# Parts of the weights' conversion and of k's low half move from VectorE to GpSimd, in short pieces

## The chip, the cores and the metric

The kernel runs on one NeuronCore of a Trainium2 chip. The metric is the device time of one execution in microseconds (us), as the median of several runs. In the profile the engines are PE (TensorE, matmuls), PEld (its weight loads), DVE (VectorE), ACT (ScalarE), POOL (GpSimd) and SP (SyncE, which here only issues DMAs). Each engine works through a queue of its own, strictly in order; semaphores make it wait for the others.

## The reference

Eight batches of attention with 8 heads, 576 positions and 64 columns a head, and behind it a gated MLP. All inputs are float32 in the reference; the two large weights arrive as 64-bit floats, and the kernel reads them as pairs of 32-bit words.

```python
scores = scale * np.matmul(q, k.transpose(0, 1, 3, 2))
cum = np.cumsum(np.maximum(s, 0.0), axis=-1)
bias = -(cum[:, :, :, None] - cum[:, :, None, :])
scores = np.where(causal, -1e9, scores + np.minimum(bias, 0.0))
attn = softmax(scores)                    # max taken off, + 1e-9 under the sum
x = np.matmul(attn, v)                    # heads side by side: 576 x 512
h = np.maximum(x @ w_in, 0.0)             # 512 -> 1024
u, v = h[..., :512], h[..., 512:]
v_n = (v - mean) / sqrt(var + 1e-6)
v_s = einsum('ts,bsd->btd', w_spatial, v_n) + b_spatial
out = (u * v_s) @ w_out                   # 512 -> 512
```

## The kernel before, in words

**Tiling.** Two heads make a pair, four pairs a batch: 32 pairs and 8 MLPs. To keep float32's accuracy with 16-bit matmuls, every operand is split in a high part (the value rounded to float16) and a low part (the value less its high part), and a product is taken as high x high, high x low and low x high.

**A pair.** Its k and q are loaded as `kraw` and `qraw` (`load_raw`, one buffer each, so the next pair's load waits until the last reader of this one's is done). `split_raw` makes the parts: of k, a cast into `KB` (line 251, DVE) and the low part over it (line 255, DVE: 64 partitions x 1152 elements); of q, a cast into `QA` (line 259, ACT) and the low part `QB` (line 264, POOL, by `pieces` at line 239, four instructions of 64 x 288). The first three pairs are native: their scores are taken from `kraw` and `qraw` in float32, without parts. `s_pass` then makes the scores (PE, line 316, seven jobs a pair, into three PSUM banks), adds the mask with the row maximum (DVE, line 320), takes exp (ACT, line 326), and writes the weights' high part (ACT, line 335) and low part (DVE, line 336) into `pb`, which a DMA on SP's queue transposes into `pT` (line 341). `av_pass` multiplies `pT` with v (PE, lines 413 and 423) and splits the result into `xt` (lines 429 and 430).

**The MLP of a batch.** `vps` (PE, line 457, the gate half of w_in), its normalisation (lines 473 to 491: `hv`, BN_STATS on DVE, the inverse root `rs` in two tiny POOL instructions at lines 482 and 483, `vn`), `ups` (line 507), `sps` with w_spatial (lines 520 to 523), the gate `g` (lines 525 to 528) and `ops` with w_out (line 539).

**The weights.** They are converted once, during the first pairs, in 128-row chunks: w_in in 8 (four of the gate half, four of the other), w_out in 4, w_spatial in 4 and a tail. `split_w64` turns 64-bit words into float32 by three DVE instructions (lines 167, 168, 170), squares the upper word on ACT (line 173), sets what is too small to zero on DVE (line 174), and calls `split_w`: the high part on ACT (line 148), and the low part either on DVE (line 150) or, with a scaled copy on ACT (line 152), on POOL (line 153). Which of the two is set by the numbers N_W1 = 2, N_W2 = 1, N_W3 = 5 and N_W4 = 0: DVE makes the low part of three w_in chunks, of all w_spatial chunks and the tail; POOL that of the other five w_in chunks and the four of w_out. w_spatial comes as float32 and goes through `split_w` alone.

**The order.** `plan` gives each step a position; up to position G_END the engines other than PE keep that order among steps marked as first. Beyond that a scheduler sets the order in each queue from its own estimate of when an operand is ready, so a changed engine for one step can move others. "Row" below is a place in an engine's queue, with equal neighbours counted once.

Of the kernel before, what the change touches and what calls it, by code (L numbers as in the profile page):

```python
# [12 lines left out]
ALU = mybir.AluOpType  # L13
# [5 lines left out]
SW = 64.0  # L19
SWSP = 1024.0  # L20
# [10 lines left out]
def attn_gated_mlp(ctx, tc, qT, kT, v, s, w_in, w_spT, b_sp, w_out, outT):  # L31
    nc = tc.nc
    P = 128
# [7 lines left out]
    w_out = w_out.bitcast(U32)  # L41
# [46 lines left out]
    KB = [cp.tile([P, 2, S], F16, name=f"KB{i}") for i in range(3)]  # L88
# [51 lines left out]
    wo1 = cp.tile([P, FC, DM], F16, name="wo1")  # L140
    wo2 = cp.tile([P, FC, DM], F16, name="wo2")
    ws1 = cp.tile([P, NFULL, S], F16, name="ws1")
    ws2 = cp.tile([P, NFULL, S], F16, name="ws2")
    wx1 = cp.tile([P, S], F16, name="wx1")
    wx2 = cp.tile([P, S], F16, name="wx2")

    def split_w(dst1, dst2, raw, sc, dve):
        nc.scalar.activation(dst1, raw, AF.Copy, bias=0.0, scale=sc)
        if dve:
            nc.vector.scalar_tensor_tensor(out=dst2, in0=raw, scalar=sc, in1=dst1, op0=ALU.mult, op1=ALU.subtract)  # L150
            return
        nc.scalar.activation(raw, raw, AF.Copy, bias=0.0, scale=sc)
        nc.gpsimd.tensor_tensor(out=dst2, in0=raw, in1=dst1, op=ALU.subtract)

    def fetch_w64(src, tag_s):
        st = wk.tile([P, 2 * NF], U32, tag=tag_s, bufs=1, name="wst")
        st = st.rearrange("p (f two) -> p f two", two=2)
        nc.sync.dma_start(out=st, in_=src.rearrange("p (f two) -> p f two", two=2))
        return st

    def split_w64(dst1, dst2, st, tag_t, dve):

        n = st.shape[1]
        lo, hi = st[:, 0:n, 0], st[:, 0:n, 1]
        t = wk.tile([P, S], U32, tag=tag_t, bufs=2, name="wt")[:, 0:n] if tag_t != "hv" else \
            wk.tile([P, NF], U32, tag="hv", bufs=2, name="wt")
        nc.vector.tensor_scalar(t, hi, 0x07FFFFFF, 3, op0=ALU.bitwise_and, op1=ALU.logical_shift_left)
        nc.vector.scalar_tensor_tensor(out=t, in0=hi, scalar=0xC0000000, in1=t, op0=ALU.bitwise_and,
                                       op1=ALU.bitwise_or)
        nc.vector.scalar_tensor_tensor(out=t, in0=lo, scalar=29, in1=t, op0=ALU.logical_shift_right,  # L170
                                       op1=ALU.bitwise_or)
        sq, tf = hi.bitcast(F32), t.bitcast(F32)
        nc.scalar.activation(sq, sq, AF.Square, bias=0.0, scale=1.0)
        nc.vector.scalar_tensor_tensor(out=tf, in0=sq, scalar=2.0 ** -30, in1=tf, op0=ALU.is_ge, op1=ALU.mult)
        split_w(dst1, dst2, tf, SW, dve)

    wsts = {}

# [3 lines left out]

    def load_win(hf, c):
        split_w64(win1[:, c, hf * NF:(hf + 1) * NF], win2[:, c, hf * NF:(hf + 1) * NF], wsts.pop((hf, c)),
                  "hv" if hf else "ob", c < (N_W1 if hf else N_W2))

    def load_wout(c):
        split_w64(wo1[:, c], wo2[:, c], fetch_w64(w_out[c * P:c * P + P], "wst"), "ob", c < N_W4)

    def load_wsp(c):  # L190
        st = wk.tile([P, S], F32, tag="ob", bufs=2, name="wsp_st")
        nc.sync.dma_start(out=st, in_=w_spT[c * P:c * P + P])
        split_w(ws1[:, c], ws2[:, c], st, SWSP, c < N_W3)

    def load_wtail():
        s4 = wk.tile([P, S], F32, tag="ob", bufs=2, name="wsx_st")
        nc.sync.dma_start(out=s4[0:TAIL], in_=w_spT[NFULL * P:S])
        nc.sync.dma_start(out=s4[TAIL:2 * TAIL], in_=w_spT[NFULL * P:S])
        split_w(wx1, wx2, s4, SWSP, N_W3 > 4)
        bf = wk.tile([1, S], F32, tag="ob", bufs=2, name="bf")  # L200
        bp = wk.tile([1, 3, S], F16, tag="wst", bufs=1, name="bp")
        nc.sync.dma_start(out=bf, in_=b_sp)
        nc.vector.tensor_scalar(bf, bf, SWSP * SVN / 2048.0, None, op0=ALU.mult)
        for i in range(3):
            nc.vector.tensor_copy(bp[:, i], bf)
            if i < 2:
                nc.vector.tensor_tensor(out=bf, in0=bf, in1=bp[:, i], op=ALU.subtract)
        for i in range(3):
            nc.sync.dma_start(out=wx2[TAIL + i:TAIL + i + 1], in_=bp[:, i])
# [25 lines left out]
    def pieces(eng, out, in0, in1):  # L235
        for j in range(2):
            for hf in range(2):
                c = slice(hf * TH, hf * TH + TH)
                eng.tensor_tensor(out=out[:, j, c], in0=in0[:, j, c], in1=in1[:, j, c], op=ALU.subtract)  # L239

    def split_raw(hb, nm, pr):

        p = 2 * hb + pr
        i = p % 3
        raw = raws[hb, 2 * pr, nm]
        lo, hi = slice(0, 64), slice(64, 128)
        if nm == "k":
            if p < N_CD:
                nc.scalar.copy(KA[i][hi], raw[hi])
            if p < N_KA:  # L250
                nc.vector.tensor_copy(KB[i], raw)
            else:
                nc.scalar.copy(KB[i], raw)
            eng = nc.gpsimd if p < N_KP else nc.vector
            eng.tensor_tensor(out=KB[i][lo], in0=raw[lo], in1=KB[i][lo], op=ALU.subtract)  # L255
            if p >= N_CD:
                nc.sync.dma_start(out=KA[i][hi], in_=KB[i][hi])
        else:
            (nc.scalar.copy if p < N_QA else nc.vector.tensor_copy)(QA[i][hi], raw[hi])  # L259
            if p < N_CD:  # L260
                (nc.scalar.copy if p < N_QA else nc.vector.tensor_copy)(QB[i][lo], raw[lo])
            else:
                nc.sync.dma_start(out=QB[i][lo], in_=QA[i][hi])
            pieces(nc.gpsimd, QB[i][hi], raw[hi], QA[i][hi])
# [311 lines left out]
    for p in range(4):  # L576
        l = (-20, -19, O_R2, O_R3)[p]
        if p < N_NS:
            at(l, True, native_tiles, p)
            at(l, True, native_sel, p)  # L580
            at((-19.9, -18.9, O_S2, O_S3)[p], True, native_cum, p)
        else:
            at(l, True, behind, "c", load_raw, 1, p % 2)
            for nm in "kq":
                at((0, 0, O_S2, O_S3)[p], True, split_raw, 1, nm, p % 2)
# [10 lines left out]
    for hb in range(2, NHB):  # L596
        lag = LAGS if hb < 4 else LAG
        for pr in range(2):
            at(4 * hb + 2 * pr - O_LR + (LAGR if hb < 4 else LAG), False, load_raw, hb, pr)
            at(4 * hb + 2 * pr - O_LD + lag, False, aux_rows, 2 * hb + pr)  # L600
            for n, nm in enumerate("kq"):
                at(4 * hb + 2 * pr - O_LD + lag + D_LD * n, False, split_raw, hb, nm, pr)
        at(4 * hb - O_LV + (LAGV if hb < 4 else LAG), False, fetch_v, hb)
        at(4 * hb - O_LV + (LAGV if hb < 4 else LAG), False, load_v, hb)
    for c in range(KC):
        at(O_WL + D_WL * c, False, fetch_win, 1, c)
        at(O_UL + D_UL * c, False, fetch_win, 0, c)
# [11 lines left out]
    for b in range(B):  # L619
        s0, s1 = 8 * b + O_M + LAG, 8 * b + 8 + O_M + LAG  # L620
        poss = [s0 + (s1 - s0) / NU * k for k in range(NU)]
        if b == 0:
# [5 lines left out]
            n = len(pre)  # L628
# [9 lines left out]
    for pos, _, first, fn, args in plan:  # L638
        n = len(traced)
# [46 lines left out]
```

## Time and profile before

| what | us |
|---|---|
| median of 3 runs | 735.04 (731.93 to 736.01) |
| the profiled execution | 736.15 |
| its span in the trace | 734.4 |
| busy: PE / DVE / ACT / POOL | 633.7 / 606.4 / 525.1 / 186.5 |

The profiled execution is 1.11 us over the median. Its span is the stretch from the first instruction to the last, 1.75 us less than its time. The page gives busy times by engine, the share of the span in 40 slices, and groups of instructions by line; a row of the trace's timeline gives the start, the length, the engine, the line, what is written from what, the tile's size, and in brackets the idle time ahead of it with what ended it. PE's busy time is modelled, so a full PE tells that it does not wait, not that it runs at its peak.

### The profile page before, as it was taken

How to read it: one execution, taken by the hardware profiler on the slowest of the kernel's cores; microseconds unless marked ns; L12 is line 12 of the kernel's file. 1: busy time of each engine (PE TensorE's matmuls, PEld its weight loads, DVE VectorE, ACT ScalarE, POOL GpSimd, SP SyncE). 2: the span in 40 equal slices, each digit the busy share in tenths (PEclk: the TensorE clock that was granted, in tenths of full speed). 3: DMA queues.
4: the chain of work that ended last, by engine and by line, in shares of the span. 5: the costliest groups of instructions: out<-in, count | busy, mean ns of one | idle time of the engine just before them, and what ended most of it. 6: DMA issues, size and time to landing. Idle time of an engine off the chain costs nothing. (4 is left out here: it accounts for less than half of the span.)

```text
span 734.4 us, 15985 instructions
## 1 busy us (share of the span) xinstructions
PE 633.7 (86%) x5696; PEld 408.8 (56%) x5696; DVE 606.4 (83%) x1660; ACT 525.1 (72%) x1334; POOL 186.5 (25%) x226
## 2 busy tenths in 40 slices
PE   4563737867656999999999999999999999999998
PEld 2232314634324577656765676476656765677576
DVE  8977998889998769898998999889988997872431
ACT  5975768667579568878787878788778888762322
POOL 7000464443022312233223322242224220100100
PEclk9986778988878999999999999999999999999999
DMA  8899957678989939898999699978996888450001
GB/s 200 193 203 213 216 148 160 110 169 184 212 189 188 203 70 188 185 206 137 213 185 227 133 188 168 237 160 170 189 231 163 159 170 184 84 109 34 33 12 65
DMA packets 243262, 119.10 MB, mean 162 GB/s; under 512 B 213887, under 2 KB 227373, under 8 KB 243182
## 3 DMA queue, kind: packets, MB, share of 16 engines
q1 hardware_dynamic: 243182, 118.08, 77.0%
q8 instruction: 45, 0.74, 0.4%
q14 instruction: 35, 0.29, 0.1%
HBM read 46.71 MB, written 9.44 MB: 76 GB/s over the span
## 5 line engine op out<-in xcount | busy, mean ns | idle before, releaser
L239 POOL TENSOR_TENSOR QB<-qraw,QA 64x288 f16<-64x288 f32 x116 | 127.5, 1129 | 321.3 <-ACT QA L259 273.4
L326 ACT ACTIVATE p<-psS,mx 128x512 f32<-128x512 f32 (+3 forms) x256 | 132.7, 524 | 50.7 <-DVE mx L320 27.0
L320 DVE CUSTOM_DVE_ANT_0 psS<-psS,mb 128x128 f32<-128x128 f32 (+3 forms) x320 | 154.2, 492 | 16.5 <-PE psS L316 13.8
L336 DVE SCALAR_TENSOR_TENSOR pb<-p,sm,pb 128x384 f16<-128x384 f32 (+3 forms) x256 | 136.3, 566 | 10.5 <-ACT pb L335 9.6
L335 ACT ACTIVATE pb<-p,sm 128x384 f16<-128x384 f32 (+3 forms) x256 | 122.7, 554 | 21.2 <-DVE sm L331 9.9
L539 PE MATMUL ops<-g,wo 128*128 128x288 f16 x768 | 108.1, 290 | 10.2 <-DVE g L525 4.4
L413 PE MATMUL av<-pT,V 128*64 128x128 f16 (+2 forms) x960 | 84.5, 294 | 34.1 <-DMA pT<-pb 28.6
L457 PE MATMUL vps<-win,xt 128*128 128x512 f16 (+1 forms) x576 | 102.7, 352 | 12.7 <-ACT p L326 7.7
L520 PE MATMUL sps<-ws,vn 128*128 128x288 f16 x768 | 108.4, 289 | 0.7 <-DVE vn L491 0.7
L507 PE MATMUL ups<-xt,win 128*128 128x288 f16 x768 | 102.4, 287 | 0.0
L316 PE MATMUL psS<-KA,QA 128*128 128x128 f16 (+3 forms) x348 | 85.4, 316 | 13.4 <-ACT p L326 11.8
L539 PEld LDWEIGHTS <-wo 128*128 128x128 f16 x768 | 74.5, 99 | 37.5 <-issue 12.0
L316 PE MATMUL psS<-KB,QB 128*128 128x128 f16 (+4 forms) x348 | 89.8, 312 | 0.4 <-DVE KB L255 0.4
L413 PEld LDWEIGHTS <-V 128*64 128x64 f16 x960 | 52.0, 116 | 66.4 <-issue 48.0
L520 PEld LDWEIGHTS <-vn 128*128 128x128 f16 x768 | 74.3, 99 | 26.3 <-issue 2.9
L507 PEld LDWEIGHTS <-win 128*128 128x128 f16 x768 | 73.4, 98 | 23.3 <-issue 2.4
L457 PEld LDWEIGHTS <-xt 128*128 128x128 f16 (+1 forms) x576 | 46.9, 103 | 60.6 <-issue 20.7
L482 POOL TENSOR_SCALAR rs<-mv 128x1 f32<-128x1 f32 x40 | 12.4, 310 | 168.1 <-DVE mv L481 154.3
L316 PEld LDWEIGHTS <-QA 128*128 128x128 f16 (+1 forms) x348 | 29.4, 102 | 39.6 <-issue 32.1
L326 ACT ACTIVATION_READ_ACCUMULATOR p<-psS,mx 128x1 f32 x256 | 51.3, 201 | 0.0
L527 ACT CAST g<-g 128x288 f16<-128x288 f32 x64 | 27.3, 427 | 31.6 <-DVE g L525 31.5
L255 DVE TENSOR_TENSOR KB<-kraw,KB 64x1152 f16<-64x1152 f32 x29 | 45.7, 1576 | 0.2
(117 smaller groups left out, 876.8 us busy)
## 6 DMA issues: line engine op xcount, KB each, us to landing
kraw<-in_kT_dram SPq DMA_DIRECT2D x61, 288.0 KB
qraw<-in_qT_dram SPq DMA_DIRECT2D x35, 288.0 KB
out_dram<-ob SPq DMA_DIRECT2D x32, 288.0 KB
vraw<-in_v_dram SPq DMA_DIRECT2D x16, 512.0 KB
wst<-in_w_in_dram SPq DMA_DIRECT2D x8, 512.0 KB
QB<-QA SPq DMA_DIRECT2D x26, 144.0 KB
KA<-KB SPq DMA_DIRECT2D x26, 144.0 KB
vraw<-in_v_dram SPq DMA_DIRECT2D x16, 128.0 KB
```

What stands on the lines that cost most here:

```text
L239: eng.tensor_tensor(out=out[:, j, c], in0=in0[:, j, c], in1=in1[:, j, c], op=ALU.subtract)
L255: eng.tensor_tensor(out=KB[i][lo], in0=raw[lo], in1=KB[i][lo], op=ALU.subtract)
L316: nc.tensor.matmul(ps[m, c0:c0 + w], U[i][:, g, q0:q0 + n], T[i][:, g, k0:k0 + w], start=st, stop=not st)
L320: nc.vector.tensor_tensor_reduce(out=ps[:, c0:c0 + w], in0=ps[:, c0:c0 + w], in1=mask, op0=ALU.add, op1=ALU.min, scale=-0.125, scalar=3.0e ...
L326: nc.scalar.activation(p32, ps[:, c0:c0 + w], AF.Exp, bias=mx[:, col:col + 1], scale=-1.0, accum_out=sm[:, acc:acc + 1])
L335: nc.scalar.activation(dst[:, off:off + w], p32, AF.Copy, bias=0.0, scale=sm[:, col:col + 1])
L336: nc.vector.scalar_tensor_tensor(out=dst[:, n + off:n + off + w], in0=p32, scalar=sm[:, col:col + 1], in1=dst[:, off:off + w], op0=ALU.mul ...
L413: nc.tensor.matmul(dst, V[i][:, jc, h + j], rhs, start=jc == n == 0 and q0 > 0, stop=jc == 3 and n == 2)
L457: nc.tensor.matmul(ps[m, 0:w], xx[:, c, t * P:t * P + (m.stop - m.start)], ww[:, c, NF + g * w:NF + g * w + w], start=c == n == 0, stop=c ...
L507: nc.tensor.matmul(ps[:, 0:TH], ww[:, c, fs], xx[:, c, ts], start=n == 0, stop=n == 3 * KC - 1)
L520: nc.tensor.matmul(ps[:, 0:TH], vv[:, c, fs], ww[:, c, ts], start=n == 0, stop=False)
L539: nc.tensor.matmul(ps[:, 0:TH], ww[:, f, ms], gg[:, f, ts], start=n == 0, stop=n == 3 * FC - 1)
```

## The change

Three things are moved. In `split_w64`, the step that sets small values to zero goes from DVE (one instruction for two operations) to POOL: a TENSOR_SCALAR that makes a factor of 0 or 64 of the square (in place, 128 x 512), and a multiplication in two halves of 128 x 256. The scale is now in the value, so the copy on ACT for the high part needs no scale, and the scaled copy of line 152 goes; the low part is always made on POOL, in two halves. The five low parts of w_spatial and its tail go from DVE to POOL, whole (128 x 576), with a scaled copy on ACT each. The low part of k goes to POOL for pairs 3 to 7 (those of the first eight that are not native) by `pieces`, four instructions of 64 x 288. Lines behind the edits stand 5 to 7 further down.

```diff
-    def split_w64(dst1, dst2, st, tag_t, dve):
+    def split_w64(dst1, dst2, st, tag_t):
...
         sq, tf = hi.bitcast(F32), t.bitcast(F32)
         nc.scalar.activation(sq, sq, AF.Square, bias=0.0, scale=1.0)
-        nc.vector.scalar_tensor_tensor(out=tf, in0=sq, scalar=2.0 ** -30, in1=tf, op0=ALU.is_ge, op1=ALU.mult)
-        split_w(dst1, dst2, tf, SW, dve)
+        nc.gpsimd.tensor_scalar(sq, sq, 2.0 ** -30, SW, op0=ALU.is_ge, op1=ALU.mult)
+        h = n // 2
+        for c in (slice(0, h), slice(h, n)):
+            nc.gpsimd.tensor_tensor(out=tf[:, c], in0=sq[:, c], in1=tf[:, c], op=ALU.mult)
+        nc.scalar.copy(dst1, tf)
+        for c in (slice(0, h), slice(h, n)):
+            nc.gpsimd.tensor_tensor(out=dst2[:, c], in0=tf[:, c], in1=dst1[:, c], op=ALU.subtract)
...
-        split_w(ws1[:, c], ws2[:, c], st, SWSP, c < N_W3)
+        split_w(ws1[:, c], ws2[:, c], st, SWSP, False)
...
-        split_w(wx1, wx2, s4, SWSP, N_W3 > 4)
+        split_w(wx1, wx2, s4, SWSP, False)
...
-            eng = nc.gpsimd if p < N_KP else nc.vector
-            eng.tensor_tensor(out=KB[i][lo], in0=raw[lo], in1=KB[i][lo], op=ALU.subtract)
+            if p < 8:
+                pieces(nc.gpsimd, KB[i][lo], raw[lo], KB[i][lo])
+            else:
+                nc.vector.tensor_tensor(out=KB[i][lo], in0=raw[lo], in1=KB[i][lo], op=ALU.subtract)
```

**POOL's queue** from the first row behind the set-up. In the names, `QB` and `KB` are the low parts of q and k, `win` and `win_117` the parts of w_in, `wt` a converted chunk; the number behind a name is its buffer. Before, rows 23 to 29:

```order
L239 TENSOR_TENSOR QB_100<-qraw_224,QA_73 64x288 x4
L239 TENSOR_TENSOR QB_101<-qraw_524,QA_74 64x288 x4
L153 TENSOR_TENSOR win_117<-wt,win_116 128x512
L239 TENSOR_TENSOR QB_102<-qraw_606,QA_75 64x288 x4
L153 TENSOR_TENSOR win_117<-wt,win_116 128x512 x2
L239 TENSOR_TENSOR QB_100<-qraw_720,QA_73 64x288 x4
L153 TENSOR_TENSOR win_117<-wt,win_116 128x512
```

And now, from the same row:

```order
L244 TENSOR_TENSOR QB_100<-qraw_224,QA_73 64x288 x4
L244 TENSOR_TENSOR KB_103<-kraw_223,KB_103 64x288 x4
L174 TENSOR_SCALAR wst<-wst 128x512 x2
L177 TENSOR_TENSOR wt<-wst,wt 128x256 x4
L174 TENSOR_SCALAR wst<-wst 128x512 x2
L180 TENSOR_TENSOR win_117<-wt,win_116 128x256 x4
L177 TENSOR_TENSOR wt<-wst,wt 128x256 x4
L244 TENSOR_TENSOR KB_104<-kraw_526,KB_104 64x288 x4
L244 TENSOR_TENSOR QB_101<-qraw_527,QA_74 64x288 x4
L174 TENSOR_SCALAR wst<-wst 128x512
L180 TENSOR_TENSOR win_117<-wt,win_116 128x256 x4
L174 TENSOR_SCALAR wst<-wst 128x512
```

Sixteen short instructions on weights now stand between pair 3's parts and pair 4's, where there was none; the queue up to pair 7's q grows from rows 23 to 32 to rows 23 to 50.

**DVE's queue** around the first MLP's first normalisation (BN_STATS of `hv_0`; `psS` with `mx` is a score job's mask and maximum, in two instructions). Before, it stands at row 213, between the first jobs of pair 5, whose second job follows:

```order
L477 BN_STATS st_0_1063<-hv_0_1061 128x6
L320 ISA psS_1086,mx_1073<-psS_1086,mb 128x512
L320 ISA mx_1073 128x1
L167 TENSOR_SCALAR wt<-wst 128x512
L477 BN_STATS st_1_1096<-hv_1_1094 128x6
```

Now it stands at row 283, among the jobs of pair 6:

```order
L327 ISA psS_1546,mx_1347<-psS_1546,mb 128x128
L327 ISA mx_1347 128x1
L484 BN_STATS st_0_1096<-hv_0_1094 128x6
L385 TENSOR_TENSOR mx_1347<-mx_1347 128x1
L484 BN_STATS st_1_1129<-hv_1_1127 128x6
```

Scores have moved ahead (pair 7's first job from row 342 to 306, pair 11's from 541 to 514, pair 13's from 660 to 600) and the first MLP back; from pair 14 on the queue has the old sequence.

**PE's queue** at the second batch's MLP. Before, its first `vps` stands at row 2312, behind only the first of pair 11's seven score jobs (the second stands at row 2336):

```order
L539 MATMUL ops_31_2405<-g_0_661,wo_118 128x288
L539 LDWEIGHTS wo_119
L539 MATMUL ops_31_2405<-g_0_660,wo_119 128x288
L457 LDWEIGHTS xt_1_1352
L457 MATMUL vps_0_2439<-win_116,xt_1_1352 128x512
```

Now it stands at row 2620; ahead of it, rows 2537 to 2544 show the last scores of pair 12 and the first of pair 13:

```order
L323 LDWEIGHTS QB_100
L323 MATMUL psS_3369<-KB_103,QB_100 128x256
L430 LDWEIGHTS V_1_107
L430 MATMUL avt_2518<-pT('t', 11)_2951,V_1_107 64x64
L323 LDWEIGHTS QA_74
L323 MATMUL psS_3424<-KA_77,QA_74 128x128
L323 LDWEIGHTS QB_101
L323 MATMUL psS_3424<-KB_104,QB_101 128x128
```

All jobs of pairs 11 and 12 have moved ahead of the second MLP. From the first matmul of the third MLP's `vps_1` on (row 3566 in both queues) the same work stands behind the same row, with neighbours swapped here and there.

More of the change, by code (lines that the diff above doesn't have):

```diff
@@ L184, in load_win @@
         split_w64(win1[:, c, hf * NF:(hf + 1) * NF], win2[:, c, hf * NF:(hf + 1) * NF], wsts.pop((hf, c)),
-                  "hv" if hf else "ob", c < (N_W1 if hf else N_W2))
+                  "hv" if hf else "ob")
     def load_wout(c):
-        split_w64(wo1[:, c], wo2[:, c], fetch_w64(w_out[c * P:c * P + P], "wst"), "ob", c < N_W4)
+        split_w64(wo1[:, c], wo2[:, c], fetch_w64(w_out[c * P:c * P + P], "wst"), "ob")
     def load_wsp(c):
```

## The prediction

> **What bounds the kernel now.** I read the time by stages first (busy us of each engine in a stretch, with the number of instructions).
>
> ```profile
> core 0: us, PE busy (x) PEld busy (x) DVE busy (x) ACT busy (x) POOL busy (x), PEclk, DMA share, GB/s
> 64.00:146.00 82.00, 52.23 (x419) 30.41 (x418) 74.88 (x160) 61.08 (x133) 35.29 (x33) 0.79 0.73 169
> 146.00:240.00 94.00, 60.06 (x528) 37.06 (x529) 86.32 (x232) 68.61 (x178) 25.78 (x23) 0.82 0.89 190
> 240.00:316.00 76.00, 76.00 (x677) 49.72 (x676) 63.98 (x172) 54.16 (x139) 20.94 (x25) 1.00 0.79 164
> 316.00:600.00 284.00, 279.89 (x2686) 184.22 (x2685) 259.39 (x748) 230.36 (x603) 81.72 (x101) 1.00 0.91 184
> ```
>
> From 240 us on PE never waits; there nothing but PE's work counts. Up to 240 us PE is idle a third of the time, and DVE is busy 161 of 176 us (92%). So the end is set by when PE becomes full, and by what it has done until then. The waits of the first 245 us tell what PE waits for (us in total, times, longest):
>
> ```profile
> PE av L413 <- DMA pT<-pb: 27.2, 12, 5.6
> DVE psS L320 <- PE psS L316: 7.2, 6, 2.5
> DVE KB L251 <- DMA kraw<-in_kT_dram: 6.0, 4, 1.9
> ```
>
> It waits for transposed weights, which hang on DVE's low parts (L336); DVE waits for others little. DVE bounds the early stage, PE the rest. All of the change lies in the early stage.
>
> **What leaves DVE.** The groups of the first 245 us, by shape (busy us, mean ns of one):
>
> ```profile
> L255 DVE TENSOR_TENSOR KB<-kraw,KB 64x1152 f16<-64x1152 f32 x11 | 18.2, 1659 | 0.0
> L174 DVE SCALAR_TENSOR_TENSOR wt<-wst,wt 128x512 f32<-128x512 f32 x12 | 9.0, 764 | 0.0
> L150 DVE SCALAR_TENSOR_TENSOR ws<-wsp_st,ws 128x576 f16<-128x576 f32 x4 | 4.0, 994 | 0.0
> L150 DVE SCALAR_TENSOR_TENSOR win<-wt,win 128x512 f16<-128x512 f32 x3 | 2.0, 673 | 0.0
> ...
> L153 POOL TENSOR_TENSOR win<-wt,win 128x512 f16<-128x512 f32 x5 | 6.5, 1305 | 6.3 <-ACT wt L152 6.2
> L153 POOL TENSOR_TENSOR wo<-wt,wo 128x512 f16<-128x512 f32 x4 | 6.2, 1561 | 14.2 <-ACT wt L152 14.1
> L239 POOL TENSOR_TENSOR QB<-qraw,QA 64x288 f16<-64x288 f32 x43 | 50.8, 1211 | 127.3 <-ACT QA L259 102.1 <-issue 24.8 <-POOL rs L483 0.3
> ```
>
> Twelve L174 (9.0 us), four L150 of w_spatial (4.0) and a tail that I take as one more (1.0), three L150 of w_in (2.0), and five of the eleven L255 (5 x 1.66 = 8.3): **24.3 us off DVE**. ACT loses nine scaled copies and gains five; being busy 130 of 176 us it isn't the bound, and I cost that at nothing.
>
> **What comes to POOL.** A piece of 64 x 288 takes 1.2 us on average here. For a half of 128 x 256 I take 1.1 us, a little below that piece; for the TENSOR_SCALAR over 128 x 512, which before doesn't have, 1.0 us (bounds: near nothing, and 1.3, the two-input pass over as many elements); for 128 x 576 1.5 us. So 12 x 1.0 + 48 x 1.1 + 5 x 1.5 + 20 x 1.2 = 96 us, less the nine L153 (12.7): **84 us more POOL**, mostly ahead of 240 us, where it had 61 in the two stages. Being idle it has the room, but not for free:
>
> ```profile
> 99.59 4.91 POOL L239 TENSOR_TENSOR QB<-qraw,QA 64x288 f16<-64x288 f32 x4 [1.99 <-ACT QA L259]
> 104.58 1.15 POOL L153 TENSOR_TENSOR win<-wt,win 128x512 f16<-128x512 f32 x1
> ...
> 99.68 1.88 DVE L255 TENSOR_TENSOR KB<-kraw,KB 64x1152 f16<-64x1152 f32 x1
> 101.49 1.21 DVE L174 SCALAR_TENSOR_TENSOR wt<-wst,wt 128x512 f32<-128x512 f32 x1
> 102.63 1.28 DVE L150 SCALAR_TENSOR_TENSOR ws<-wsp_st,ws 128x576 f16<-128x576 f32 x1
> 103.84 0.42 DVE L320 CUSTOM_DVE_ANT_0 psS<-psS,mb 128x256 f32<-128x256 f32 x1
> ...
> 127.21 0.72 DVE L150 SCALAR_TENSOR_TENSOR ws<-wsp_st,ws 128x576 f16<-128x576 f32 x1
> ```
>
> ```profile
> L174 DVE SCALAR_TENSOR_TENSOR wt<-wst,wt x12: 651/676/1214, 66.5 to 219.7; 128x512 f32<-128x512 f32 x12
> ```
>
> ```profile
> L255 DVE TENSOR_TENSOR KB<-kraw,KB x29: 1331/1351/2301, 15.6 to 596.7; 64x1152 f16<-64x1152 f32 x29
> ```
>
> While POOL runs (99.6 to 105.7), DVE's instructions with two inputs in SBUF take 1.88, 1.21 and 1.28 us, where they take 1.35, 0.68 (the middle numbers, the medians) and 0.72 otherwise: 1.6 us lost in 6.1 us of POOL. L320, whose first input is in PSUM, loses nothing. A second place, on the L336 that stay on DVE:
>
> ```profile
> 203.89 3.63 POOL L239 TENSOR_TENSOR QB<-qraw,QA 64x288 f16<-64x288 f32 x4 [14.21 <-issue]
> ...
> 204.44 2.50 DVE L336 SCALAR_TENSOR_TENSOR pb<-p,sm,pb 128x384 f16<-128x384 f32 x3 [0.26 <-ACT pb L335]
> 206.86 1.88 DVE L255 TENSOR_TENSOR KB<-kraw,KB 64x1152 f16<-64x1152 f32 x1
> ...
> 217.22 1.53 DVE L336 SCALAR_TENSOR_TENSOR pb<-p,sm,pb 128x384 f16<-128x384 f32 x3
> ```
>
> 0.97 + 0.53 = 1.5 us in 3.6. Together 3.1 in 9.7: **a us of POOL costs DVE 0.32 us**. 84 x 0.32 = 27 us come back on DVE, against 24.3 that leave: +3. The short pieces don't alter this price, as nearly all of POOL's work in both places is already such a piece.
>
> The Trainium skill, SBUF — State Buffer, "Who interferes with whom", states that a DVE instruction with two SBUF inputs and a GpSimd instruction that reads SBUF exclude each other for the whole instruction. If DVE stood still for each added us, 84 - 24 would make the kernel some 60 us slower, an estimate; the rows above have a third of that price, since DVE loses only what is left of POOL's instruction when its own is due; I give that estimate no chance of its own beyond the tail of the last rival below.
>
> **POOL's queue as a path.** It is in order, and pairs 4 to 7 now wait in it behind weights. It can begin on the weights when ACT has the squares:
>
> ```profile
> 63.41 1.23 ACT L173 ACTIVATE wst<-wst 128x512 f32<-128x512 f32 x2
> ```
>
> ```profile
> 110.39 4.77 POOL L239 TENSOR_TENSOR QB<-qraw,QA 64x288 f16<-64x288 f32 x4 [0.32 <-POOL rs L483]
> ```
>
> From there to pair 7's q its rows hold 8 TENSOR_SCALARs, 30 halves, 32 pieces and one 128 x 576: 8 + 33 + 38.4 + 1.5 = 81 us, so pair 7's low parts are done at 64.6 + 81 = 146 us; before, that was 115 for q. Behind pair 7's last piece wait the first MLP's two `rs`, and DVE's `hv_0` behind those. DVE comes to the same place at about the same time: pair 7's scores stand at row 306 of its queue now, and before it passed its row 305 at 148.5 us (first line); what fewer long instructions ahead of that row free, the added POOL takes again:
>
> ```profile
> 148.46 0.55 DVE L320 CUSTOM_DVE_ANT_0 psS<-psS,mb 128x384 f32<-128x384 f32 x1
> ...
> 161.14 0.28 DVE L320 CUSTOM_DVE_ANT_0 psS<-psS,mb 128x128 f32<-128x128 f32 x1
> ...
> 243.88 0.29 DVE L320 CUSTOM_DVE_ANT_0 psS<-psS,mb 128x128 f32<-128x128 f32 x1
> ```
>
> Pair 7's first score job was at 161.1 (second line), pair 11's at 243.9 (third): 82.7 us for 199 rows, 0.416 us a row. I take 146 for pair 7 now. From there to pair 11 the new order has 208 rows, 86.5 us at the same pace; the w_out chunks add some 26 us of POOL there (8 us of DVE) and take four L174 off (3 us): 146 + 86.5 + 5 = **237.5 us, 6 us earlier than before**.
>
> **What the order does to PE.** At pair 11's first job PE is at row 2200 (2228 before). Before, it went on at once to the second MLP, which needs nothing of pair 11:
>
> ```profile
> 245.16 2.75 PE L457 MATMUL vps<-win,xt 128*128 128x512 f16 x12
> ...
> 316.18 2.75 PE L457 MATMUL vps<-win,xt 128*128 128x512 f16 x12
> ```
>
> The first is that MLP's first matmul (row 2312), the second the third MLP's `vps_1` (row 3566): 627 matmuls in 71.0 us, 8.83 a us. Now PE must first do all jobs of pairs 11 and 12 and pair 11's `av`, which needs the last low part of pair 11's weights, DVE's row 580: 66 rows behind pair 11's first, 27.5 us. With a mean wait for a transposition (27.2 / 12 = 2.3 us) and the 22 matmuls from there to row 2620 (2.5 us) the second MLP starts at 237.5 + 32.3 = 269.8 us. Then 473 matmuls, 53.6 us: row 3566 at 323.4, against 316.2. PE idles in that stretch, as row 2200 to 2620 is only 210 matmuls, 24 us of work in 32. **Sum: +7.2 us**, and from there both do the same with a full PE, DVE being idle 25 us of 284 (the stage from 316 us). The profiled 736.15 becomes 743.4; the same on the median gives 742. I predict **743 us**.
>
> **Rivals.**
> *DVE's relief comes through.* If POOL's pieces fall between DVE's conflicts and POOL's queue runs at its fastest pieces,
>
> ```profile
> 88.70 3.49 POOL L239 TENSOR_TENSOR QB<-qraw,QA 64x288 f16<-64x288 f32 x4 [2.82 <-ACT QA L259]
> ...
> 139.48 8.37 POOL L239 TENSOR_TENSOR QB<-qraw,QA 64x288 f16<-64x288 f32 x4 [6.28 <-issue]
> ```
>
> (3.49 / 4 = 0.87 us, first line, and the rest in proportion), POOL is through by 64.6 + 81 x 0.87 / 1.2 = 123, and pair 7 hangs on DVE alone. The added 57 us of POOL up to there (81 less 24 that it had) then cost nothing instead of 18, and the 8 behind are gone too: +7 - 26 = -19, at most. With half of that cost left -6, with a quarter left -12. I set this case at 727. For it: DVE really loses 24 us, and 92% busy on the bound engine. Against it: the rows show the conflict in every burst of POOL.
> *Nothing changes*, 735: the same with slightly over half the price; conflict and relief cancel, and PE loses nothing by the order since the first MLP is late by no more than the pairs are early.
> *POOL becomes the bound.* By the second line pieces can take 2.1 us, when DVE wins most turns. If a quarter of the 70 instructions up to pair 7 go so (0.9 us more each, 16 us), DVE stands waiting for KB, QB and `rs` and can't make use of its time: 743 + 14 = 757. It decides from where POOL's queue is later than DVE's own arrival, 146 to 149 us, so there is no slack for it.
> That the edits do not do what they say is no rival: the queues show them.
>
> **How the numbers follow.** Forecast, 739 to 750: 0.38. POOL as the bound, above 750: 0.12. Relief, below 731: 0.30. Nothing, 731 to 739: 0.20. Within 0.5% (3.7 us, about what a measurement of this kernel can tell from no change) is 0.20, faster 0.30, slower 0.50. Leaving a tenth on either side, the range is 723 to 757.
>
> **What would show it.** Right: DVE as busy up to 240 us as now though it has 25 instructions fewer; groups of three L336 nearer to 2.5 than to 1.5 us from 65 to 150 us; pair 7's first L327 near 146; POOL nearly gapless from 65 to 146; the second MLP's first matmul near 270 and PE full only from there. Wrong: that matmul ahead of 258, or POOL's halves at 0.8 us and below, which would let the relief through; or DVE waiting on POOL's KB or `rs` for many us, which would make it slower still.

## The result, and the profile after

| | median, us | range | ratio to before (95%) |
|---|---|---|---|
| before, beside it | 735.52 | 731.93 to 738.17 | |
| after | 759.81 | 757.75 to 761.83 | 1.0333 (1.028 to 1.0386) |

The change makes the kernel 24 us (3.3%) slower. The profiled execution of after took 760.26 us, its span 758.5. Its engines' busy times over the whole span (share, instructions):

```profile
PE 648.9 (86%) x5696; PEld 413.3 (54%) x5696; DVE 607.0 (80%) x1635; ACT 524.6 (69%) x1330; POOL 260.3 (34%) x302
```

DVE is as busy as before (606.4) with 24 us of instructions fewer, POOL 73.8 us busier. The stages of after, with the columns of the table of before:

```profile
core 0: us, PE busy (x) PEld busy (x) DVE busy (x) ACT busy (x) POOL busy (x), PEclk, DMA share, GB/s
64.00:146.00 82.00, 45.91 (x345) 21.51 (x344) 69.31 (x146) 57.20 (x131) 76.58 (x78) 0.71 0.79 172
146.00:240.00 94.00, 65.64 (x558) 41.32 (x558) 87.91 (x218) 67.85 (x169) 51.14 (x44) 0.82 0.84 180
240.00:316.00 76.00, 65.49 (x496) 42.29 (x493) 53.77 (x140) 45.41 (x114) 22.64 (x28) 0.87 0.70 144
316.00:600.00 284.00, 279.12 (x2663) 182.20 (x2661) 249.49 (x716) 223.32 (x582) 76.05 (x96) 1.00 0.85 175
```

Two things stand out. POOL is busy 76.58 of 82 us between 64 and 146 (before 35.29). And the stage from 240 to 316, in which PE was full before (677 matmuls), now has 496 matmuls, with DVE at 53.77 of 76: neither engine is full there. From 64 to 240 PE has 903 matmuls now and had 947, from 240 to 316 it has 496 and had 677: most of the loss lies behind 240. Over the whole span the same 5696 matmuls keep PE busy for 648.9 us (before 633.7), so of the 24.1 us of span 15.2 are longer matmuls and 8.9 more idle time, a rough split, as PE's busy times are modelled. The longer matmuls go with a lower granted clock (PEclk, 0.87 from 240 to 316 where it was 1.00). What PE does there (timeline; in brackets its idle time ahead of the row and what ended it):

```profile
238.66 2.83 PE L420 MATMUL av<-pT,V 128*64 128x384 f16 x22 [5.64 <-DMA pT<-pb]
...
247.56 1.62 PE L546 MATMUL ops<-g,wo 128*128 128x288 f16 x6 [3.52 <-ACT wo L178]
...
259.32 3.36 PE L420 MATMUL av<-pT,V 128*64 128x384 f16 x29 [3.38 <-DMA pT<-pb]
...
279.13 2.75 PE L464 MATMUL vps<-win,xt 128*128 128x512 f16 x12
...
338.73 2.76 PE L464 MATMUL vps<-win,xt 128*128 128x512 f16 x12
```

The second MLP's first matmul comes at 279.13 (before 245.16), the third MLP's `vps_1`, row 3566, at 338.73 (before 316.18). Up to 279 PE has only the attention of pairs 10 to 13, one transposition after another, and the first MLP's `ops`, which wait for w_out's converted chunks (second row). PE's own waits that end with a part of w_in or w_out are short, 5.8 us in all from 64 us to the second MLP (before 8.2): what is late with the chunks is the work that would fill the waits for transpositions. The DMA engines are about as busy as before (share 0.92 from 240 to 280 us, before 0.89 from 200 to 245). These chunks are the end of a path that runs through the whole early stage. Before (timeline of POOL and of SP's queue: last low part of w_in, first load of w_out, last low part of w_out):

```profile
118.90 1.31 POOL L153 TENSOR_TENSOR win<-wt,win 128x512 f16<-128x512 f32 x1 [2.47 <-ACT wt L152]
...
152.31 0.37 SPq L158 DMA_DIRECT2D wst<-in_w_out_dram  x1
...
228.22 1.16 POOL L153 TENSOR_TENSOR wo<-wt,wo 128x512 f16<-128x512 f32 x1
```

And after:

```profile
143.06 1.30 POOL L180 TENSOR_TENSOR win<-wt,win 128x256 f16<-128x256 f32 x2
...
191.34 0.52 SPq L158 DMA_DIRECT2D wst<-in_w_out_dram  x1
...
263.48 1.30 POOL L180 TENSOR_TENSOR wo<-wt,wo 128x256 f16<-128x256 f32 x2
```

The lateness is 24 us at the end of w_in, 39 at w_out's first load, 35 at its last part and 34 at the second MLP. Between w_in and w_out the staging buffers (those that hold a weight between its load and its conversion) lead through w_spatial and the bias: `wst`, w_out's only staging buffer, is also that of the bias pieces `bp`, and these come behind w_spatial's tail in the two buffers `ob`, which w_out's converted chunk `wt` shares too.

### The profile page after: what moved, and what is told of

The parts are those of the page before. It is cut to its first block, busy times and chain, and to the rows that moved or that the text cites. A ratio compares the mean times of both kernels' runs of the same rounds, so it can differ in the third digit from the quotient of the medians.

```text
span 758.5 us, 16050 instructions
## 1 busy us (share of the span) xinstructions
PE 648.9 (86%) x5696; PEld 413.3 (54%) x5696; DVE 607.0 (80%) x1635; ACT 524.6 (69%) x1330; POOL 260.3 (34%) x302
## 5 line engine op out<-in xcount | busy, mean ns | idle before, releaser
L244 POOL TENSOR_TENSOR QB<-qraw,QA 64x288 f16<-64x288 f32 x116 | 119.6, 1060 | 231.5 <-ACT QA L266 180.6
L333 ACT ACTIVATE p<-psS,mx 128x128 f32<-128x128 f32 (+3 forms) x256 | 132.5, 523 | 56.0 <-DVE mx L327 35.1
L343 DVE SCALAR_TENSOR_TENSOR pb<-p,sm,pb 128x384 f16<-128x384 f32 (+3 forms) x256 | 141.5, 590 | 7.9 <-ACT pb L342 7.6
L420 PE MATMUL av<-pT,V 128*64 128x128 f16 (+2 forms) x960 | 88.5, 300 | 43.5 <-DMA pT<-pb 37.7
L323 PE MATMUL psS<-KA,QA 128*128 128x128 f16 (+5 forms) x348 | 90.0, 331 | 29.0 <-ACT p L333 20.1
L527 PE MATMUL sps<-ws,vn 128*128 128x288 f16 x768 | 106.2, 287 | 0.9 <-ACT u L517 0.7
L323 PE MATMUL psS<-KB,QB 128*128 128x128 f16 (+4 forms) x348 | 94.1, 324 | 1.1 <-POOL QB L244 1.0
L420 PEld LDWEIGHTS <-V 128*64 128x64 f16 x960 | 53.9, 118 | 75.0 <-issue 55.3
L546 PEld LDWEIGHTS <-wo 128*128 128x128 f16 x768 | 73.8, 98 | 33.0 <-issue 7.5
L527 PEld LDWEIGHTS <-vn 128*128 128x128 f16 x768 | 73.8, 98 | 24.7 <-issue 3.3
L323 PEld LDWEIGHTS <-QB 128*128 128x128 f16 (+1 forms) x348 | 31.1, 107 | 34.9 <-issue 25.8
```

The source lines that it names most:

```text
L323: nc.tensor.matmul(ps[m, c0:c0 + w], U[i][:, g, q0:q0 + n], T[i][:, g, k0:k0 + w], start=st, stop=not st)
L333: nc.scalar.activation(p32, ps[:, c0:c0 + w], AF.Exp, bias=mx[:, col:col + 1], scale=-1.0, accum_out=sm[:, acc:acc + 1])
L343: nc.vector.scalar_tensor_tensor(out=dst[:, n + off:n + off + w], in0=p32, scalar=sm[:, col:col + 1], in1=dst[:, off:off + w], op0=ALU.mul ...
L420: nc.tensor.matmul(dst, V[i][:, jc, h + j], rhs, start=jc == n == 0 and q0 > 0, stop=jc == 3 and n == 2)
L527: nc.tensor.matmul(ps[:, 0:TH], vv[:, c, fs], ww[:, c, ts], start=n == 0, stop=False)
L546: nc.tensor.matmul(ps[:, 0:TH], ww[:, f, ms], gg[:, f, ts], start=n == 0, stop=n == 3 * FC - 1)
```

## The experiments

Three theories. **Weights**: the path above sets the time, POOL's full queue makes it late. **Order**: the scheduler's new order, with the jobs of pairs 11 to 13 ahead of the second MLP, sets it. **Contention**: DVE bounds the early stage, and what counts is its work, less what left, plus what POOL's accesses cost it.

The medians of before in the four batches were 735.5 to 740.2, so the ratio is what is to be compared. The other columns are from each run's trace, in us: end of w_in's last low part, first load of w_out, end of its last low part, first matmul of the second MLP.

| run | median | before | ratio (95%) | w_in | w_out from | to | 2nd MLP |
|---|---|---|---|---|---|---|---|
| before | 735.52 | | 1 | 120.2 | 152.3 | 229.4 | 245.2 |
| after | 759.81 | 735.52 | 1.0333 (1.028 to 1.0386) | 144.4 | 191.3 | 264.8 | 279.1 |
| e1_k_alone | 736.29 | 739.99 | 0.9969 (0.9934 to 1.0005) | 125.1 | 156.0 | 230.9 | 247.9 |
| e2_wsp_alone | 733.62 | 739.99 | 0.9916 (0.9886 to 0.9945) | 121.4 | 156.0 | 223.7 | 238.3 |
| e3_w64_alone | 750.25 | 739.99 | 1.0135 (1.0089 to 1.0181) | 128.9 | 176.9 | 248.3 | 263.6 |
| e4_after_zero_dve | 738.90 | 739.99 | 1.0002 (0.998 to 1.0024) | 131.1 | 159.8 | 226.6 | 247.3 |
| e5_after_order | 755.86 | 737.37 | 1.0253 (1.0219 to 1.0287) | 143.7 | 191.1 | 258.2 | 266.1 |
| e6_after_bp | 750.75 | 737.37 | 1.0174 (1.0135 to 1.0213) | 144.7 | 141.4 | 247.1 | 262.8 |
| e7_before_bp | 731.76 | 737.37 | 0.9938 (0.9906 to 0.997) | 120.2 | 104.8 | 217.6 | 231.8 |
| e8_after_wout_old | 752.99 | 737.37 | 1.0207 (1.0173 to 1.0241) | 144.7 | 191.7 | 253.2 | 268.5 |
| e9_after_k_dve | 746.45 | 739.92 | 1.0083 (1.0045 to 1.0122) | 138.8 | 175.8 | 247.5 | 260.8 |
| e10_after_whole | 759.55 | 739.92 | 1.0267 (1.0164 to 1.0371) | 143.7 | 188.9 | 257.6 | 275.0 |
| e11_after_bp_wout_old | 746.88 | 739.92 | 1.0081 (1.0048 to 1.0113) | 144.6 | 141.3 | 245.0 | 259.8 |
| e12_wsp_bp | 725.13 | 739.92 | 0.9786 (0.9714 to 0.9859) | 123.1 | 105.4 | 210.8 | 227.1 |
| e13_after_wo_free | 728.77 | 740.20 | 0.9853 (0.9813 to 0.9893) | 145.7 | | | 230.8 |
| e14_before_wo_free | 719.07 | 740.20 | 0.9720 (0.9675 to 0.9766) | 125.2 | | | 206.6 |
| e15_after_wsp_dve | 757.85 | 740.20 | 1.0275 (1.0217 to 1.0332) | 137.9 | 186.5 | 257.1 | 273.9 |
| e16_wsp_bp_k | 737.07 | 740.20 | 0.9953 (0.991 to 0.9997) | 130.6 | 102.0 | 226.1 | 240.0 |

The last two columns go together: the second MLP starts 13 to 18 us behind w_out's last low part wherever w_out is converted, but for e4 (21) and e5 (8, where the order was held).

### Each part alone, and the zeroing undone

k's pieces alone, in before:

```diff
-            eng = nc.gpsimd if p < N_KP else nc.vector
-            eng.tensor_tensor(out=KB[i][lo], in0=raw[lo], in1=KB[i][lo], op=ALU.subtract)
+            if p < 8:
+                pieces(nc.gpsimd, KB[i][lo], raw[lo], KB[i][lo])
+            else:
+                nc.vector.tensor_tensor(out=KB[i][lo], in0=raw[lo], in1=KB[i][lo], op=ALU.subtract)
```

> Before with only k's low part of pairs 3 to 7 on POOL in pieces. Weights theory (the second MLP starts some 15 us behind the last low part of w_out, the weights go one after another through few staging buffers, and POOL's queue delays w_in): POOL gets 16 us of pieces between 65 and 140 us, w_in's five low parts there wait a piece or two longer, w_in done a few us later than before's 120 us; second MLP's first vps 245 to 250, time 735 to 739. Contention theory (only DVE's work counts): 8.3 us leave DVE, 16 x 0.3 = 5 come back, 732 or so. Order theory (the place of the second MLP in PE's queue sets it): row 2340 instead of 2312, so 735 to 737.

w_spatial alone, in before:

```diff
-        split_w(ws1[:, c], ws2[:, c], st, SWSP, c < N_W3)
+        split_w(ws1[:, c], ws2[:, c], st, SWSP, False)
...
-        split_w(wx1, wx2, s4, SWSP, N_W3 > 4)
+        split_w(wx1, wx2, s4, SWSP, False)
```

> Before with only w_spatial's five low parts on POOL, whole, with their scaled copies on ACT. Weights theory: w_spatial's chunks go through two staging buffers and each is held a copy and a wait for POOL longer, so w_out's first load is some 5 us later than before's 152 us, second vps at 248 to 252, time 737 to 740. Contention theory: 5 us leave DVE, 7.5 x 0.3 = 2.3 come back: 732. Order theory: row 2280, a little ahead of before: 733 to 735.

The 64-bit weights alone (after with the two edits above taken back):

```diff
-        split_w(dst1, dst2, tf, SW, dve)
+        nc.gpsimd.tensor_scalar(sq, sq, 2.0 ** -30, SW, op0=ALU.is_ge, op1=ALU.mult)
...
```

> Before with only the new conversion of the 64-bit weights (w_in and w_out): zeroing in three POOL instructions, low parts always on POOL in halves. Weights theory: this is what fills POOL (some 8 x 6.3 us for w_in), so it has most of the loss: w_in done at about 135 us, second vps 258 to 268, time 744 to 752. Contention theory: 11 us leave DVE, some 50 x 0.3 = 15 come back: 739. Order theory: row 2466, half way between before's 2312 and after's 2620: 745.

After with the zeroing on DVE:

```diff
-        nc.gpsimd.tensor_scalar(sq, sq, 2.0 ** -30, SW, op0=ALU.is_ge, op1=ALU.mult)
-        h = n // 2
-        for c in (slice(0, h), slice(h, n)):
-            nc.gpsimd.tensor_tensor(out=tf[:, c], in0=sq[:, c], in1=tf[:, c], op=ALU.mult)
-        nc.scalar.copy(dst1, tf)
+        nc.vector.scalar_tensor_tensor(out=tf, in0=sq, scalar=2.0 ** -30, in1=tf, op0=ALU.is_ge, op1=ALU.mult)
+        nc.scalar.activation(dst1, tf, AF.Copy, bias=0.0, scale=SW)
+        nc.scalar.activation(tf, tf, AF.Copy, bias=0.0, scale=SW)
+        h = n // 2
```

> After with the zeroing back on DVE in one instruction a chunk, the scale back in two copies on ACT; the low parts of all weights and of k stay on POOL. Weights theory: POOL loses 12 x (2.23 + 2.04) = 51 us, w_in is done near 125 us, second vps at 248 to 254, time 735 to 742. Contention theory: DVE gets 9 us, loses 51 x 0.3 = 15 us less: 754. Order theory: row 2286, as before: 735.

k alone changes nothing that can be told; w_spatial alone is faster, which the weights theory had wrong (its second MLP is 7 us earlier, not later) and contention had in the right direction; the 64-bit weights alone cost 1.35%. With the zeroing back on DVE the loss is gone, where contention expected 754: it falls as the main cause. (Its w_in, at 131, is later than the weights theory's 125.) Weights and order fit e3 and e4 alike; the order held, below, tells them apart. The three parts multiply to 1.0019, and together they cost 1.0333. Busy times of e3 and then of e4 in the stage up to 146 us (same columns as above; POOL is the fifth):

```profile
64.00:146.00 82.00, 49.44 (x347) 25.11 (x347) 75.90 (x152) 57.69 (x125) 70.70 (x66) 0.67 0.80 182
```

```profile
64.00:146.00 82.00, 50.72 (x382) 26.89 (x376) 67.19 (x152) 65.28 (x142) 58.60 (x64) 0.78 0.78 180
```

The 64-bit weights alone take POOL to 70.70 of 82 us. What is added then has no room, and w_in is done at 129 (e3), 138 (e15, with k), 139 (e9, with w_spatial) and 144 us (all).

### One part undone

After with k on DVE (the first diff taken back), and after with w_spatial on DVE (the second):

> After with k's low part back on DVE; weights and w_spatial as in after. Weights theory: POOL's queue is 16 us shorter up to 140 us, so w_in is done at 130 to 136 instead of 144, w_out's last low part at 250 to 256, second vps 15 us behind at 265 to 271, time 749 to 755. If the parts add up as they do alone (w_spatial 0.9916, the 64-bit weights 1.0135): 1.005, some 739 to 741.

> After with w_spatial's low parts back on DVE; the 64-bit weights and k as in after. Alone, this part made before faster. If it costs in after since w_spatial's staging buffers are held until the full POOL queue comes to them (w_spatial done at 163 us, 18 us behind w_in): w_spatial done at 150 to 155, w_out's first load at 180 to 185, second vps at 268 to 274, time 750 to 755. If it helps in after as it does alone: 764 to 768.

Taking k back returns 2.5% of the 3.33%, more than the weights theory expected (on 735.5 the ratio 1.0083 is 742, the second MLP 4 us ahead of the range): without k, w_spatial and the 64-bit weights nearly add up as they do alone (a product of 1.005). Taking w_spatial back returns 0.6%, which the intervals don't tell from nothing, with the second MLP in the range expected. k and the 64-bit weights together cost 1.0275 where their product is 1.0104. So k, free alone, costs beside the 64-bit weights. That it does so because POOL's queue is full there is the likely reading and not shown: e16, below, has k cost without a full queue.

### The order held

PE's queue gets a fixed order at one place: all score jobs of pairs 11 to 13 but the first behind the second MLP's first matmul.

```diff
+            if gen is mlp and args[0] == 1 and k == 0:
+                held[0] = pe[0].name
+            if gen is s_pass and held and (args[0] > 11 or args[0] == 11 and k >= 1):
+                for x in pe:
+                    tc.add_manual_dep(x, held[0], nosync, reason="pace")
```

> After with PE's queue held so that all score jobs of pairs 11 to 13, but pair 11's first, stand behind the second MLP's first vps (row 2498 instead of 2620); nothing is taken away. Order theory (the jobs of pairs 11 to 13 ahead of the second MLP cost the time): second vps at 255 to 262, time 745 to 750. Weights theory (the second MLP stands behind the first one's ops, these behind the last low part of w_out at 265 us): PE waits in the same place for the same chunk, second vps at 272 to 280, time 755 to 762.

The second MLP is 13 us earlier, the kernel only 0.8% faster (some 6 us; the intervals of the two ratios touch). Its PE in the stages 240 to 280 and 280 to 316:

```profile
240.00:280.00 40.00, 31.35 (x241) 19.92 (x239) 17.29 (x34) 14.86 (x31) 11.83 (x18) 0.79 0.46 119
280.00:316.00 36.00, 36.00 (x292) 26.00 (x289) 31.37 (x94) 25.84 (x71) 9.61 (x11) 1.00 0.58 113
```

After itself has 227 matmuls in the first stage, before 326. Doing the MLP first leaves the attention undone: PE is still idle for over a fifth of the stage up to 280, with w_out's last part at 258. The order theory's 745 to 750 is missed; by the medians the order is worth about a quarter of the loss. The weights theory had the time nearly right (on 735.5 the ratio is 754) and the second MLP too late: a part of the first MLP's `ops` moved behind it.

### w_out brought forward

The bias pieces in a buffer of their own, in after and in before:

```diff
-            bp = wk.tile([1, 3, S], F16, tag="wst", bufs=1, name="bp")
+            bp = wk.tile([1, 3, S], F16, tag="bp", bufs=1, name="bp")
```

> After with the three pieces of the spatial bias in a buffer of their own, so that w_out's first load no longer waits until these pieces are through with the staging buffer that both share (bias done at 185 us, first load of w_out at 191 us). Weights theory: first load of w_out 20 to 50 us earlier, its last low part at 235 to 250 us, second vps 15 us behind, at 250 to 265, time 740 to 752. If the first MLP itself (its vps, ups and sps, 33 to 40 us later than before) is the late one and not w_out, less than 4 us change: 756 to 760. Order theory: row 2498, as in the run with the order held.

> Before with the same edit. Weights theory: first load of w_out well ahead of 152 us, last low part at 215 to 222 instead of 229, second vps at 231 to 238, time 4 to 8 us under before's. If w_out's lateness sets nothing in before, as before.

The edit moves no work to another engine, and both are faster, by 1.6% and 0.6% of before's time, as the weights theory expected. e6 has its second MLP at the same row of PE's queue as e5 (2498) and is 0.8% faster than that, with intervals that do not touch; as the place is the same, this difference is hard to put down to the order. In e6 (timeline of SP's queue, POOL and PE):

```profile
141.40 0.58 SPq L158 DMA_DIRECT2D wst<-in_w_out_dram  x1
...
244.52 2.62 POOL L180 TENSOR_TENSOR wo<-wt,wo 128x256 f16<-128x256 f32 x2 [2.38 <-ACT wo L178]
...
262.82 2.75 PE L464 MATMUL vps<-win,xt 128*128 128x512 f16 x12
```

Of the 50 us by which the load is earlier, 18 reach the last part and 16 the second MLP. The rest is lost ahead of the conversion: DVE's first step on w_out (line 167) is at 178.55 us, only 17 us earlier than in after (195.86). It comes 1.9 us behind the end of w_spatial's tail on POOL (176.64), which fits the code: w_out's `wt` takes one of the two `ob` buffers.

w_out the old way in after, alone and with this edit (`split_w64` is here the function of before, `split_n64` that of after):

```diff
-        split_w64(win1[:, c, hf * NF:(hf + 1) * NF], win2[:, c, hf * NF:(hf + 1) * NF], wsts.pop((hf, c)),
+        split_n64(win1[:, c, hf * NF:(hf + 1) * NF], win2[:, c, hf * NF:(hf + 1) * NF], wsts.pop((hf, c)),
...
-        split_w64(wo1[:, c], wo2[:, c], fetch_w64(w_out[c * P:c * P + P], "wst"), "ob")
+        split_w64(wo1[:, c], wo2[:, c], fetch_w64(w_out[c * P:c * P + P], "wst"), "ob", c < N_W4)
```

> After with w_out converted the old way (zeroing on DVE, scaled copy on ACT, low part whole on POOL) and w_in the new way. Weights theory: w_out's own conversion takes as long in both kernels (77 us from first load to last low part before, 74 after), only its start is late, and this edit comes behind the start: last low part at 258 to 265, second vps at 273 to 280, time 753 to 760. If the slow POOL steps of w_out cost it, four chunks x 8 us of POOL: second vps at 255 to 265, time 742 to 750.

> After with both edits on w_out (bias pieces in a buffer of their own, w_out converted the old way); w_in, w_spatial and k as in after. Weights theory with w_out's last chunk as the only link that counts: last low part at 230 to 238, second vps at 246 to 253, time 736 to 742. If the first MLP itself, 33 to 40 us late since w_in is, comes to bound next: second vps not ahead of 256, time 744 to 750.

e8 falls between the two expectations: from the same first load the last part is 12 us earlier, so w_out's own POOL steps do cost something. With both edits the loss is down to 0.8%, but w_out is still the last link (the first MLP's `ops` wait 1.90 us at 245.05 for its last part), at 245 and not at 238, though its first load is at 141. The start is late, not the pace: DVE's first step on it is at 179.08, again 1.9 us behind w_spatial's tail, and from there to the last part it takes 66 us, where before takes 73.

### w_out left out

In both kernels w_out's parts are copied from w_in's, so nothing waits for its load and conversion.

```diff
     def load_wout(c):
-        split_w64(wo1[:, c], wo2[:, c], fetch_w64(w_out[c * P:c * P + P], "wst"), "ob")
+        nc.scalar.copy(wo1[:, c], win1[:, c, 0:NF])
+        nc.scalar.copy(wo2[:, c], win2[:, c, 0:NF])
```

> After without w_out's load and conversion (its two parts are copied on ACT from the converted w_in, so the product is of the wrong weights; this is left out). If w_out's last chunk is what the second MLP waits for in after: second vps at 240 to 250, time 730 to 740. If the first MLP itself, late by w_in, bounds as much: not ahead of 255, time 743 or more.

> Before without w_out's load and conversion, in the same way. If w_out's last chunk is what the second MLP waits for in before too: second vps at 215 to 225, time 712 to 722. If not: second vps at 238 to 245 and time 728 to 733, the difference being the work that is left out.

After falls by 4.8% (1.0333 to 0.9853), before by 2.8%. In e13 PE does more in the stage up to 240 (after 558 matmuls) and is nearly full up to 280 (after 227 matmuls):

```profile
146.00:240.00 94.00, 76.17 (x623) 48.39 (x624) 81.66 (x216) 70.07 (x178) 33.66 (x34) 0.89 0.85 175
240.00:280.00 40.00, 38.04 (x378) 25.76 (x377) 35.64 (x99) 30.34 (x78) 12.13 (x14) 1.00 0.80 155
```

The second MLP starts at 230.8 and in e14 at 206.6, both earlier than expected, in e13 with w_in as late as in after (145.7). The two kernels without w_out are 1.3% apart (0.9853 against 0.9720, some 10 us), with it 3.3%: **about 15 of the 24 us go with w_out**. The other 10 stay without it; that they come from the first MLP itself, late behind w_in (its first `ops` are at 211 us in e13 and at 182 in e14), is likely and was not tested alone. The split is a rough one: the work left out also frees DVE, ACT and POOL, and the scheduler moves the second MLP ahead (1178 matmuls run before it in e13 and 1077 in e14; 1366 in after, 1212 in before), so the order's share is in it. In e7 it moves too (1158); e6 against e5 (1305 and 1304) is the comparison at one place.

### Whole pieces, and a faster version

After with each new POOL instruction whole:

```diff
-        for c in (slice(0, h), slice(h, n)):
-            nc.gpsimd.tensor_tensor(out=tf[:, c], in0=sq[:, c], in1=tf[:, c], op=ALU.mult)
+        nc.gpsimd.tensor_tensor(out=tf, in0=sq, in1=tf, op=ALU.mult)
...
-        for c in (slice(0, h), slice(h, n)):
-            nc.gpsimd.tensor_tensor(out=dst2[:, c], in0=tf[:, c], in1=dst1[:, c], op=ALU.subtract)
+        nc.gpsimd.tensor_tensor(out=dst2, in0=tf, in1=dst1, op=ALU.subtract)
...
-                pieces(nc.gpsimd, KB[i][lo], raw[lo], KB[i][lo])
+                nc.gpsimd.tensor_tensor(out=KB[i][lo], in0=raw[lo], in1=KB[i][lo], op=ALU.subtract)
```

> After with every new POOL subtraction and multiplication whole instead of in halves or quarters. Weights theory: POOL's elements are the same and its queue as long or a little shorter, second vps at 270 to 279, time 752 to 760. If the short pieces cost (overheads, more turns at DVE's port): 740 to 750. If they save: 764 or more.

The size of the pieces makes no difference that the intervals tell. Before with the two edits that were faster alone, and then with k as well:

> Before with the two edits that made it faster by themselves: w_spatial's low parts on POOL and the bias pieces in a buffer of their own. If the two add up: 0.9916 x 0.9938 = 0.985, some 726, second vps at 224 to 232. If both shorten the same wait: 0.990, 730 to 732.

> Before with w_spatial's low parts on POOL, the bias pieces in their own buffer, and k's low part of pairs 3 to 7 on POOL in pieces. If k's move is free as long as POOL is not full: 722 to 726, as without it or a little less. If it delays w_in's low parts in POOL's queue (125 instead of 123 us) and w_out behind them: 727 to 732; second vps 5 us later than the 227 us without it.

```profile
208.87 1.93 POOL L153 TENSOR_TENSOR wo<-wt,wo 128x512 f16<-128x512 f32 x1 [1.23 <-ACT wt L152]
...
227.12 2.75 PE L457 MATMUL vps<-win,xt 128*128 128x512 f16 x12
```

These rows of e12 show w_out done 19 us and the second MLP begun 18 us earlier than before; it is 2.1% faster than before (1.4 to 2.9%), no less than the two edits promised, and beats both kernels. k's move costs most of that again (0.9953): w_in is 7 us later, w_out 15, the second MLP 13. So k's move is not free even where POOL is busy for less than two thirds of the time (50 of 82 us up to 146 in e16). The rows show what it holds up: w_spatial's tail stands on POOL behind four pieces of q that start at 156.74, and ends at 163.44 (in e12 at 141.24); DVE's first step on w_out follows 1.7 us behind it in both runs, at 165.15 and 142.94.

## Where the prediction held and where it failed

The direction was right, but the size was not: 743 us was forecast and 759.81 measured, outside the range of 723 to 757, and most of the loss came by a way that the sum does not have. By its steps:

- **What bounds.** That the end is set by when PE becomes full, and by its work up to then, held nearly: the loss is 22.6 us at row 3566 and 24.1 at the end of the span. That DVE bounds the early stage did not: e7 takes no work off DVE and is faster than before, and e1 takes 5.7 us of busy time off it (606.4 to 600.7) with no change that can be told.
- **24.3 us off DVE, a us of POOL costs 0.32.** Both held, as far as busy times tell. DVE's is 0.6 us more with 24.3 less to do and 73.8 more on POOL: (24.3 + 0.6) / 73.8 = 0.34. In the same way e1 gives 0.28 (8.3 leave, the busy time falls by 5.7, POOL has 9.4 more), e2 0.28 and e3 0.25. The forecast's net +3 is +0.6. The Trainium skill, SBUF — State Buffer, "SBUF: two separate sides", has the engine that comes second block for the whole of the other one's instruction; no run here shows a price near one us per us.
- **84 us more on POOL.** It was 73.8. The groups of after (busy us, mean ns of one):

```profile
L174 POOL TENSOR_SCALAR wst<-wst 128x512 f32<-128x512 f32 x12 | 26.8, 2233 | 53.0 <-DMA pT<-pb 42.8 <-ACT wst L173 8.2 <-issue 1.4
L177 POOL TENSOR_TENSOR wt<-wst,wt 128x256 f32<-128x256 f32 x24 | 24.5, 1045 | 0.8 <-DVE sm L338 0.4
L244 POOL TENSOR_TENSOR KB<-kraw,KB 64x288 f16<-64x288 f32 x20 | 15.2, 784 | 0.1
L180 POOL TENSOR_TENSOR win<-wt,win 128x256 f16<-128x256 f32 x16 | 13.9, 896 | 0.3
```

The TENSOR_SCALAR took 2.23 us where 1.0 was taken and 1.3 was the upper bound, k's pieces 0.78 instead of 1.2, w_in's halves 0.90 instead of 1.1. By luck the errors cancel: all that came to POOL took 96.7 us, for 96 in the sum. The 10 us less come mostly from q's pieces, which took 119.6 us over the whole run and 127.5 before.

- **POOL's queue.** Nearly gapless up to pair 7's q, as forecast, and through earlier (rows of POOL):

```profile
62.83 5.43 POOL L174 TENSOR_SCALAR wst<-wst 128x512 f32<-128x512 f32 x2 [42.76 <-DMA pT<-pb]
...
135.77 3.06 POOL L244 TENSOR_TENSOR QB<-qraw,QA 64x288 f16<-64x288 f32 x4 [1.55 <-issue]
...
140.78 1.14 POOL L489 TENSOR_SCALAR rs<-mv 128x1 f32<-128x1 f32 x2 [1.94 <-DVE mv L488]
```

It is through at 138.8 us instead of 146. Pair 7's and pair 11's first score jobs on DVE:

```profile
149.38 0.28 DVE L327 CUSTOM_DVE_ANT_0 psS<-psS,mb 128x128 f32<-128x128 f32 x1
...
242.49 0.30 DVE L327 CUSTOM_DVE_ANT_0 psS<-psS,mb 128x128 f32<-128x128 f32 x1 [2.17 <-PE psS L323]
```

They come at 149.4 for 146 and 242.5 for 237.5: pair 11 is 1.4 us earlier than before, not 6.

- **The step that failed: "What the order does to PE".** It let the second MLP wait for pair 11's last low part and one transposition, 32.3 us behind pair 11's first job, at 269.8. It starts at 279.1. It was right that it comes behind the jobs of pairs 11 and 12, but that order is worth about a quarter of the loss (e5). What it stands behind is the first MLP's `ops`, and these behind w_out's last chunk, done 14 us before it; some 15 of the 24 us go with w_out (e13, e14). The step before it had left this out: "POOL's queue as a path" followed k and q and the two `rs` through the queue and left out the weights themselves, on which the whole change lies; w_out's chunks had a term of 5 us for their load on the engines and none for when they begin. The lateness of w_in, w_spatial and the bias was in view in the queues, and e6, e13 and e14 show that it carries over. With the cause mistaken, a sum that comes within 9.3 us of the second MLP is in part luck.
- **The sum.** +7.2 forecast at row 3566, +22.6 measured: 5.0 at pair 11's first job, 4.3 from there to the second MLP, and 6.0 behind it, where 473 matmuls at the mean rate of before took 59.6 and not 53.6 us. PE is full in that stretch at a clock of 1.00, so the rate was mis-sized: more of these matmuls are the MLP's (390 of 475 in the trace, where the stretch of before has 391 of 630). The sum costs PE at this rate of the full clock from pair 11's first job on and has no term for the clock, which is 0.74 on average from 240 to 279 us; what that took by itself no run here separates.
- **The rivals.** POOL as the bound, given 0.12, comes nearest, with 757 (its price of 16 us stands in its sum as 14, without a reason given). That the number is so near is luck: DVE hardly waited for KB, QB and `rs` (1.2 us for `rs` from 60 to 180 us), and POOL was through with them earlier than DVE came. It cost through the weights.

## What to carry to other kernels

When work moves to an engine with idle time, follow every chain that now passes through its queue to the last consumer, conversions done once and their staging buffers too; average idleness says nothing of a queue that is full for 80 us. A part that is harmless alone (k, 0.997) can cost 2.5% beside another in one queue, so try the parts alone and together. A buffer shared by two unrelated steps is worth a look first: giving the bias its own made both kernels faster.

## What was not expected of the hardware

A one-input TENSOR_SCALAR with two operations on POOL, in place on every second 32-bit word (128 x 512), took 2.23 us on average (12 of them, 1.96 at the least), more than the two-input pass over as many elements (1.31 for w_in and 1.56 for w_out in before). The granted clock of PE goes with its idle time: after has 0.71, 0.82 and 0.87 in the stages with waits and 1.00 behind 316. It falls from 1.00 to 0.50 at 236.0 us, 3.0 us into the wait of 5.64, and again, after 3.5 us at 1.00, at 246.3, 2.2 us into the one of 3.52, and stays at 0.50 until 263.3. There matmuls are slower: two score matmuls of 128 x 512 start 0.39 us apart at 254.5 and 0.22 us apart at 263.4. So a wait costs more than its own length. The Trainium skill, TensorE: Matmul & The Clock Gate, Part 1, has the clock fall after an idle window of about 3.4 us. The first fall, 3.0 us into a wait, is near that, the second, at 2.2 us, is earlier, and no run here tests the threshold.
